# Loading one head of k first in a fused attention and mixer kernel: a smaller first load, a smaller memset, and the row chain put behind

## The chip, the cores and the metric

The kernel runs on one core of one Trainium2 chip. The metric is the device time of one execution in microseconds (us). Engines are called by their names in the profile: PE is TensorE's matmuls, PEld its weight loads, DVE is VectorE, ACT is ScalarE, POOL is GpSimd, SP is SyncE, which here only issues DMAs.

## The reference

Grouped-query attention over 8 batches, 16 query heads that share 4 key and value heads, 384 tokens of 64 elements; its output, turned to tokens by 1024, goes through a residual MLP mixer.

```python
scores = (1/sqrt(64)) * q @ k^T            # k, v repeated 4 times over the heads
attn   = softmax(scores)
x      = (attn @ v) as [8, 384, 1024]
a1  = alpha1 * x + beta1
tok = einsum('ts,bsd->btd', w_tok, a1)      # w_tok 384 x 384
u   = x + lam * tok
a2  = alpha2 * u + beta2
ch  = relu(a2 @ w_ch1) @ w_ch2              # 1024 -> 4096 -> 1024
out = u + lam * ch
```

All inputs and the output are float32.

## The kernel before, in words

The work is split by batch. Batch 0 goes through attention and token mixing alone, in a lead-in of some 36 us (`side(0)`), while weights are still being loaded; from then on TensorE works on the two large matmuls of one batch (or of two together) and takes the attention of a later batch in between. The order of instructions on every engine is the order in which the program writes them (`manual_schedule`): each engine takes its own from that one text, in that order, and an engine that waits holds up all that stands behind it on the same engine. The tile framework adds the semaphore waits.

The lead-in is what the change touches. Its pieces:

- **Warm-up.** `wtokT` is cleared by VectorE (L847), and PE multiplies it with itself (`warmup`, L844): nine matmuls of 384 columns before anything is loaded, three more after the first scores, one after the fourth. Their results are not used.
- **Loads.** SP issues, in this order: heads 0 and 1 of k (`load_k`, L150), the row alpha1 and the row lam (`load_row`, L869), heads 2 and 3 of k, then the rows beta1, alpha2 and beta2. ScalarE issues q of heads 0 to 3 in two halves (L879). GpSimd issues the other q heads (L884), v (L164), w_tok (L944) and, after those, the weights w_ch1 (L185). GpSimd's own row work (`split` for beta) and its copies of heads 2 and 3 stand behind the first two loads of w_ch1.
- **k.** `place_k` (L160) copies a head of k twice, side by side, into bf16. For heads 0 and 1 of batch 0 one copy is VectorE's and the other ScalarE's. `k_transpose` (L255 on PE, copied by VectorE at L257) turns a head of k into `kT`; `q_transpose` (L265, copied at L267) does the same for q, two heads to a pair.
- **Scores and exponentials.** `scores` (L279) fills a PSUM bank, of which there are two, in 18 steps of four 128 x 128 blocks for two heads each; ScalarE takes the exponential of each step (L288). Nine blocks make one pair of heads, so steps 0 to 2 need pairs 0 and 1 only, and step 4 is the first that needs pair 2 (its q and head 1 of k).
- **av.** `av_piece` (L315) multiplies by v; VectorE divides by the row sums (L320, L323).
- **Row chain.** VectorE multiplies alpha1 by lam (`scale_rows`, L903) and splits the product into bf16 parts (`split`, L911, L913, L919). `spread` (L396 on PE, copied to `vecs` by VectorE, L398) hands these rows to all 128 partitions, and `a1` (L334) multiplies x by them.
- **w_tok.** `wtok_transpose` (L369, copied by VectorE, L372) turns w_tok into `wtokT`, three blocks at a time; the third of them waits for a PSUM bank that the copy of the first one frees.

`at` in `side(0)` lists what follows each step of scores: the number is the step, and the pieces are written out in the order of the list.

Of the kernel before, what the change touches and what calls it, by code (L numbers as in the profile page):

```python
# [12 lines left out]
def kernel(  # L13
# [21 lines left out]
    nc = tc.nc  # L35
    f32 = mybir.dt.float32
# [7 lines left out]
    B, Hq, S, D = q.shape  # L44
    Hkv = k.shape[1]
# [3 lines left out]
    P = 128  # L49
    NST = S // P  # L50
# [30 lines left out]
    hTf = hT.rearrange("p n s -> p (n s)")  # L81
# [45 lines left out]
    wtokT = const.tile([P, NST, S], bf, tag="wtokT", name="wtokT")  # L127
# [5 lines left out]
    ks, k2s, qrs = {}, {}, {}  # L133

    def by_head(ap):
        return ap.rearrange("h (p st) d -> p h st d", st=NST)

    def k_tile(b):
        k2s[b] = sb.tile([P, Hkv, 2, NST, D], bf, tag="k2", name="k2", bufs=1)

    def load_k(b, hs=(0, 2)):
        if b > 1:
            k_tile(b)
            for a in range(2):
                nc.gpsimd.dma_start(out=k2s[b][:, :, a], in_=by_head(k[b]))
            return
        for h in hs:
            ks[b, h // 2] = t = hTf[:, 7680 + 384 * h:8448 + 384 * h].bitcast(f32).rearrange(
                "p (h st d) -> p h st d", h=2, st=NST)
            nc.sync.dma_start(out=t, in_=by_head(k[b, h:h + 2]))  # L150

    def place_k(b, i, hs=(0, 1)):
        if b not in k2s:
            k_tile(b)
        copies = [nc.gpsimd.tensor_copy] * 2
        if b == 1 or b == 0 == i:
            copies = (nc.vector.tensor_copy, nc.vector.tensor_copy if i else nc.scalar.copy)
        lo, hi = hs[0], hs[-1] + 1
        for a in range(2):
            copies[a](out=k2s[b][:, 2 * i + lo:2 * i + hi, a], in_=ks[b, i][:, lo:hi])  # L160
# [22 lines left out]
    def load_w1(c):  # L183
        w1_slots[c] = w1_free.pop(0)
        nc.gpsimd.dma_start(out=w1[:, w1_slots[c]], in_=w1src[:, :, c * CW * P:(c + 1) * CW * P])  # L185
# [5 lines left out]
    def bank(shape, tag, name, dtype=f32):  # L191
        if tag == "mm":
            return mms.tile(shape, dtype, tag="mm", name=name, bufs=2)
        return psum.tile(shape, dtype, tag=tag, name=name, bufs=2 if tag == "sc" else 1)
# [34 lines left out]
    def side(b):  # L229
# [172 lines left out]
        def add(f, *a):  # L402
            us.append(lambda: f(*a))
# [28 lines left out]
        if not first:  # L432
# [10 lines left out]
            if (b - NPL) // 2 > 0:  # L443
                at = {}
# [18 lines left out]
                **{39 + 4 * i - i // 2 * 2: [(turn, p)] for i, p in enumerate((5, 6, 7)) if by_pe(p)}}  # L463
        add(k_transpose, 0, 1)
        add(q_transpose, 0, 1, "av", "ACT")
        add(place_k, 0, 0, (1,))
        add(q_transpose, 1, 1, "tp")
        lower, upper = range(NP // 2), range(NP // 2, NP)
        ut = a2_transpose
        at = {0: [(warmup, 3), (scale_rows, 0), (split, 0, 1, 0)], 1: [(k_transpose, 1, 1)],  # L470
              2: [(q_transpose, 2, 2, "av"), (split, 0, 1, 1)], 3: [(warmup, 1)],
              4: [(av, 0)], 5: [(spread, lower, "tp"), (a1, 0)], 6: [(av, 1), (k_transpose, 2, 2, "tp")],
              7: [(q_transpose, 4, 2, "av"), (a1, 1)], 8: [(av, 2)],
              9: [(wtok_transpose, 0, "av"), (wtok_transpose, 1, "tp")],
              10: [(wtok_transpose, 2, "av"), (q_transpose, 6, 2, "mm"), (fill_h, 0)], 11: [(av, 3), (rows_r, "tp")],
# [363 lines left out]
    with tc.manual_schedule(engines=order):  # L839

        def warmup(n):
            warm = bank([P, 512], "mm", "warm")
            for _ in range(n):
                nc.tensor.matmul(out=warm[:, :S], lhsT=wtokT[:, 0, :P], rhs=wtokT[:, 1, :],  # L844
                                 start=True, stop=True)

        nc.vector.memset(wtokT, 0.0)  # L847
        warmup(9)
        load_k(0, [0])

        rows_f = hTf[:32, 9216:10496].bitcast(f32)
        rows_t = hTf[:32, 10496:11520].bitcast(f32)
# [15 lines left out]
        def load_row(i, ap, n=4):  # L868
            nc.sync.dma_start(out=rows_f[:n * NP, i * P:(i + 1) * P],  # L869
                              in_=bass.AP(tensor=ap.tensor, offset=ap.offset, ap=[[0, n], [P, NP], [1, P]]))  # L870

        load_row(0, moe_alpha1)
        load_row(3, moe_lam)
        load_k(0, [2])
        load_row(1, moe_beta1)
        load_row(2, moe_alpha2, 1)
        load_row(4, moe_beta2, 1)
# [5 lines left out]
        def load_q4(g):  # L883
            nc.gpsimd.dma_start(out=qgs[g], in_=q[0, g * G:(g + 1) * G].rearrange("h (p st) d -> p h st d", st=NST))  # L884
# [5 lines left out]
            nc.vector.memset(t[:, :, :, D:], 1.0)  # L890
        AX = mybir.AxisListType.X
        nc.vector.tensor_copy(out=ident_f, in_=ident)
        for i, m in enumerate(masks):
            nc.vector.tensor_reduce(out=m, in_=ident[:32, 8 * (i + 1):24 + 8 * (i // 2)], op=ADD, axis=AX)
        nc.vector.tensor_scalar(out=masks[2], in0=masks[2], scalar1=-1.0, scalar2=None, op0=MUL)
# [47 lines left out]
        load_q4(2)  # L943
        nc.gpsimd.dma_start(out=wtok_in, in_=moe_w_tok.rearrange("(p tt) s -> p tt s", tt=NST))  # L944
        load_q4(3)
        place_k(0, 0, (0,))
        load_w1(order1[0])
        load_w1(order1[1])
        place_k(0, 1)
        scale_rows(1, nc.gpsimd)  # L950
        split(1, 2, None, nc.gpsimd)
# [7 lines left out]
        for i, f in enumerate(side(0)):  # L959
            f()  # L960
            if i == 3:
                load_k(1)
# [16 lines left out]
        def put_flips(ps, phase, b, places):  # L979
            for u, m in zip(places, ((flip_k, b), *((flip_q, b, i, 2) for i in range(0, NP, 2)))):  # L980
                put(ps, phase, u, *m)

        turns, at = side(1)
        put_all(0, 0, turns)
        put_all(0, 1, at)
        put_flips(0, 1, 2, (34, 36, 37, 42, 43))

        put(0, 1, 45, load_next, 3)
        put_all(1, 0, side(2)[1], lambda u: int(1.5 * u))
        put_flips(1, 0, 3, (53, 55, 57, 59, 61))  # L990
        put_all(1, 1, side(3)[1])
# [68 lines left out]
```

## Time and profile before

| what | value |
|---|---|
| time, median of 3 runs | 739.87 us (739.78 to 740.77) |
| the profiled execution | 739.61 us |
| its span in the profile | 737.8 us |
| PE busy | 727.0 us, 99% |
| VectorE, ScalarE, GpSimd busy | 69%, 44%, 22% |
| first matmul on PE | 1.52 us |
| first exponential on ScalarE | 6.34 us |
| mean granted clock of TensorE | 1.00 |

A line of the timeline gives the start and the duration in us, the engine, the line of the kernel, the operation, what it writes and reads, its shape, and how many instructions were merged; in brackets stands the idle time of the engine just before and what ended it. A line of the waits gives the waiting engine and line, what it waited for, the sum in us, the number of waits and the longest. Ends of matmuls are modelled, and a q after an engine's name is its sequencer.

### The profile page before, as it was taken

Reading aid. Unit: us, or ns where it says so; the run is one execution under the profiler, and the core shown is the slowest. Engines: PE = TensorE matmul, PEld = TensorE weight load, DVE = VectorE, ACT = ScalarE, POOL = GpSimd, SP = SyncE. Lnnn points to the kernel's source line nnn. Section 1 sums busy time; section 2 is a strip of 40 time slices with the busy share of each in tenths; the row PEclk is TensorE's granted clock in tenths of the full one; section 3 lists DMA queues with packets and bytes.
Section 4 is the critical chain, followed back from the end, with each engine's and each line's share of the span. In section 5 each row is a group of like instructions: output and inputs, shape, how many; then the busy total and the mean of one; then the engine's idle time right before and its main releaser. Section 6 shows DMA issues by size and latency. Waiting matters only on the chain.

```text
span 737.8 us, 14477 instructions
## 1 busy us (share of the span) xinstructions
PE 727.0 (99%) x5710; PEld 418.6 (57%) x5769; DVE 512.0 (69%) x993; ACT 325.7 (44%) x469; POOL 164.0 (22%) x211
## 2 busy tenths in 40 slices
PE   8999999999999999999999999999999999999998
PEld 5866555666555566655555566655555556654444
DVE  7763366467587889749777988747958988762354
ACT  7632431554332566663334366664343266660000
POOL 9434221420000332301012244020002222000011
PEclk9999999999999999999999999999999999999999
DMA  9999999999999999999979999998989999837965
GB/s 188 194 202 200 207 217 179 186 198 181 219 264 260 183 226 223 249 262 215 284 186 224 178 176 165 190 250 199 276 236 167 217 149 144 149 136 241 289 184 107
DMA packets 218017, 151.31 MB, mean 205 GB/s; under 512 B 88661, under 2 KB 197061, under 8 KB 217949
## 3 DMA queue, kind: packets, MB, share of 16 engines
q0 software_dynamic: 120304, 64.60, 66.8%
q1 hardware_dynamic: 96956, 85.33, 41.5%
q8 instruction: 45, 0.74, 0.4%
q10 hardware_dynamic: 688, 0.46, 0.2%
q14 instruction: 24, 0.19, 0.1%
HBM read 154.84 MB, written 38.27 MB: 262 GB/s over the span
## 4 chain that ended last, share of the span: by engine, by line
PE 85%; DVE 6%; DMA 5%; issue 2%; POOL 2%; ACT 0%; DVEq 0%; POOLq 0%
PE C L789 25%; PE X L723 17%; PE h L532 10%; PE ch L570 10%; PE Y L723 8%; PE sc L279 4%; PE Z L723 4%; PE sc L315 3%; PE sc L340 3%; DMA q_raw<-in_q_dram 2%; DMA ops<-a 1%; DMA out_dram<-hT 1%; DVE xr L323 1%; DVE hT L826 1%; DVE xr L347 1%
## 5 line engine op out<-in xcount | busy, mean ns | idle before, releaser
L288 ACT ACTIVATE es<-sc 128x1024 bf16<-128x1024 f32 x126 | 121.4, 1024 | 154.6 <-PE sc L279 143.5
L789 PE MATMUL C<-w,arena 128*128 128x512 bf16 (+2 forms) x711 | 163.7, 372 | 1.6 <-issue 0.3
L789 PEld LDWEIGHTS <-arena 128*128 128x128 bf16 x1040 | 94.8, 98 | 100.5 <-issue 5.1
L728 ACT ACTIVATE hT<-X,bias 128x384 f32<-128x384 f32 x144 | 83.8, 582 | 63.8 <-PE X L723 56.8
L723 PEld LDWEIGHTS <-w 128*128 128x128 bf16 x768 | 75.1, 98 | 50.5 <-issue 0.7
L185 POOL DMA_DIRECT2D w<-in_moe_w_ch_dram x68 | 62.2, 926 | 125.4 <-PE Z L723 51.7
L570 PE MATMUL ch<-arena,hT 128*128 128x512 bf16 x366 | 87.9, 379 | 1.0 <-issue 0.3
L517 POOL DMA_DIRECT2D out_dram<-hT x33 | 28.8, 872 | 258.4 <-DVE hT L688 79.7
L532 PE MATMUL h<-ops,w 128*128 128x384 bf16 (+1 forms) x480 | 83.2, 327 | 0.4
L723 PEld LDWEIGHTS <-pad 128*128 128x128 bf16 x576 | 56.4, 98 | 37.2
L723 PE MATMUL X<-ops,w 128*128 128x384 bf16 x384 | 70.2, 326 | 0.0
L723 PE MATMUL X<-ops,pad 128*128 128x384 bf16 x384 | 70.2, 326 | 0.0
L789 PE MATMUL C<-pad,arena 128*128 128x512 bf16 (+2 forms) x288 | 69.5, 373 | 0.4
L532 PEld LDWEIGHTS <-w 128*128 128x128 bf16 x480 | 45.3, 98 | 30.1 <-issue 1.8
L570 PEld LDWEIGHTS <-hT 128*128 128x128 bf16 x384 | 34.7, 98 | 36.8 <-issue 2.5
L347 DVE TENSOR_TENSOR xr<-sc,xr 128x384 f32<-128x384 f32 x56 | 31.0, 553 | 24.2 <-PE sc L340 24.2
L315 PEld LDWEIGHTS <-es 128*128 128x128 bf16 x1008 | 38.2, 97 | 12.4
L340 PEld LDWEIGHTS <-wtokT 128*128 128x128 bf16 x576 | 37.5, 98 | 11.8 <-DVE a L330 0.8
L279 PE MATMUL sc<-qT,kT 64*128 64x384 bf16 (+2 forms) x576 | 41.9, 271 | 1.8 <-ACT hT L288 0.3
L320 DVE RECIPROCAL rinv<-sc 128x6 f32<-128x6 f32 x56 | 10.8, 192 | 44.3 <-PE sc L315 44.1
L315 PE MATMUL sc<-v,es 128*128 128x65 bf16 x1008 | 39.8, 193 | 0.0
L723 PE MATMUL Z<-ops,w 128*128 128x384 bf16 x192 | 39.0, 326 | 0.2
(138 smaller groups left out, 910.6 us busy)
## 6 DMA issues: line engine op xcount, KB each, us to landing
w<-in_moe_w_ch_dram POOLq DMA_DIRECT2D x68, 512.0 KB, 9.6
w<-w2s SPq DMA_DIRECT2D x60, 512.0 KB, 4.6
pad<-w2s SPq DMA_DIRECT2D x24, 512.0 KB, 7.4
out_dram<-xr SPq DMA_DIRECT2D x56, 192.0 KB, 5.3
out_dram<-hT POOLq DMA_DIRECT2D x33, 256.0 KB, 6.0
arena<-in_moe_w_ch_dram POOLq DMA_DIRECT2D x16, 512.0 KB, 20.0
w2s<-arena SPq DMA_DIRECT2D x28, 256.0 KB, 4.9
q_raw<-in_q_dram POOLq DMA_DIRECT2D x28, 192.0 KB, 9.7
```

Source lines behind the costliest of these rows:

```text
L185: nc.gpsimd.dma_start(out=w1[:, w1_slots[c]], in_=w1src[:, :, c * CW * P:(c + 1) * CW * P])
L279: nc.tensor.matmul(out=sc[:, hh, k % 4:k % 4 + n], lhsT=kT[r, 2 * p // G, BLK[hh][sk], :], rhs=qT[r, p, st:st + n, :], start=True, stop=True)
L288: nc.scalar.activation(out=e, in_=sc, func=EXP, scale=scale_qk)
L315: nc.tensor.matmul(out=av[:, hh, sq, :], lhsT=ess[k // 4][:, m % 2, k % 4, :], rhs=vb[:, sk, hk, :], start=(sk == 0), stop=(sk == NST - 1))
L340: nc.tensor.matmul(out=ps[:, tt, :], lhsT=wtokT[:, st, tt * P:(tt + 1) * P], rhs=a1s[p][:, st, :], start=(st == 0), stop=(st == NST - 1 an ...
L347: nc.vector.tensor_tensor(out=u, in0=ps, in1=u, op=ADD)
L517: nc.gpsimd.dma_start(out=at, in_=o, accum_op=ADD)
L532: nc.tensor.matmul(out=ps[:, :n], lhsT=w1[:, w1_slots[c], dt, j * P:(j + 1) * P], rhs=a2T[:, dt, :n], start=(dt == 0), stop=(dt == NDT - 1))
L570: nc.tensor.matmul(out=ps, lhsT=hT[:, nt, ms * P:(ms + 1) * P], rhs=w2[:, row(nt)[0], row(nt)[1], cs], start=(i == 0), stop=(i == NNT - 1))
L723: nc.tensor.matmul(out=ps, lhsT=tb[g, o][:, dt, e * P:(e + 1) * P], rhs=opb(LEFT1[o])[:, dt], start=(o in (1, 2, 7) and dt == 0), stop=(dt ...
L728: nc.scalar.activation(out=snap[o, e], in_=ps, func=IDENT, bias=hi if o == 5 else lo)
L789: nc.tensor.matmul(out=x, lhsT=hid[:, t, LEFT2[o], ms * P:(ms + 1) * P], rhs=rhs[:, t % 4 * 512 + c0:t % 4 * 512 + c1], start=((not last o ...
```

## The change

Four edits, all in the lead-in of batch 0:

1. Only the first third of `wtokT` is cleared by the memset, and the warm-up matmuls use that third for both operands; eight of them stand at the start in place of nine.
2. The first load of k holds head 0 alone. Head 1 gets a load of its own, behind the rows alpha1 and lam and ahead of heads 2 and 3.
3. The two copies of head 0 are written right behind the float copy of the identity, ahead of the small reductions that make the masks; the copies of head 1 stand behind both q transpositions, and both are VectorE's.
4. The first part of the row chain (`scale_rows` and the first half of `split`) is put from behind step 0 to behind step 1, after the transposition of head 1, and `spread` with the first `a1` from behind step 5 to behind step 6.

```diff
-    def load_k(b, hs=(0, 2)):
+    def load_k(b, parts=((0, 2), (2, 4))):
...
-        for h in hs:
-            ks[b, h // 2] = t = hTf[:, 7680 + 384 * h:8448 + 384 * h].bitcast(f32).rearrange(
-                "p (h st d) -> p h st d", h=2, st=NST)
-            nc.sync.dma_start(out=t, in_=by_head(k[b, h:h + 2]))
+        t = hTf[:, 7680:9216].bitcast(f32).rearrange("p (h st d) -> p h st d", h=Hkv, st=NST)
+        ks[b, 0], ks[b, 1] = t[:, :2], t[:, 2:]
+        for lo, hi in parts:
+            nc.sync.dma_start(out=t[:, lo:hi], in_=by_head(k[b, lo:hi]))
...
-            copies = (nc.vector.tensor_copy, nc.vector.tensor_copy if i else nc.scalar.copy)
+            copies = (nc.vector.tensor_copy, nc.vector.tensor_copy if i or hs == (1,) else nc.scalar.copy)
...
         add(k_transpose, 0, 1)
         add(q_transpose, 0, 1, "av", "ACT")
+        add(q_transpose, 1, 1, "tp")
         add(place_k, 0, 0, (1,))
-        add(q_transpose, 1, 1, "tp")
...
-        at = {0: [(warmup, 3), (scale_rows, 0), (split, 0, 1, 0)], 1: [(k_transpose, 1, 1)],
+        at = {0: [(warmup, 3)], 1: [(k_transpose, 1, 1), (scale_rows, 0), (split, 0, 1, 0)],
               2: [(q_transpose, 2, 2, "av"), (split, 0, 1, 1)], 3: [(warmup, 1)],
-              4: [(av, 0)], 5: [(spread, lower, "tp"), (a1, 0)], 6: [(av, 1), (k_transpose, 2, 2, "tp")],
+              4: [(av, 0)], 6: [(spread, lower, "tp"), (a1, 0), (av, 1), (k_transpose, 2, 2, "tp")],
...
-                nc.tensor.matmul(out=warm[:, :S], lhsT=wtokT[:, 0, :P], rhs=wtokT[:, 1, :],
+                nc.tensor.matmul(out=warm[:, :S], lhsT=wtokT[:, 0, :P], rhs=wtokT[:, 0, :],
                                  start=True, stop=True)
 
-        nc.vector.memset(wtokT, 0.0)
-        warmup(9)
-        load_k(0, [0])
+        nc.vector.memset(wtokT[:, 0, :], 0.0)
+        warmup(8)
+        load_k(0, ((0, 1),))
...
         load_row(0, moe_alpha1)
         load_row(3, moe_lam)
-        load_k(0, [2])
+        load_k(0, ((1, 2), (2, 4)))
...
         nc.vector.tensor_copy(out=ident_f, in_=ident)
+        place_k(0, 0, (0,))
...
         load_q4(3)
-        place_k(0, 0, (0,))
         load_w1(order1[0])
```

## The prediction

> **What bounds the kernel now.** I read the page first, then the chain of waits, then PE's waits, then the first 16 us of each engine in the timeline.
>
> ```profile
> PE 727.0 (99%) x5710; PEld 418.6 (57%) x5769; DVE 512.0 (69%) x993; ACT 325.7 (44%) x469; POOL 164.0 (22%) x211
> ```
>
> TensorE is busy 99% of 737.8 us, so only idle or slow time of PE can be won. All of PE's waits in the run:
>
> ```profile
> PE warm L844 <- DVE wtokT L847: 1.5, 1, 1.5
> ...
> PE sc L279 <- ACT hT L288: 0.3, 1, 0.3
> PE tp L369 <- DVE wtokT L372: 0.2, 1, 0.2
> PE sc L279 <- DVE xr L323: 0.2, 1, 0.2
> PE tok L344 <- DVE arena L387: 0.2, 1, 0.2
> ```
>
> Every one that matters lies in the first 20 us. By windows, PE is idle 2.15 us of 0 to 16, and 0.18 us of 16 to 40. So the end moves by what the last wait before the dense part moves: that of the third w_tok transposition (L369) at 15.56 for VectorE. VectorE's timeline says why:
>
> ```profile
> 5.94 0.56 DVE L267 CAST qT<-tp 128x384 bf16<-128x384 f32 x1 [0.47 <-PE tp L265]
> 7.20 0.28 DVE L903 TENSOR_TENSOR hT<-hT 32x128 f32<-32x128 f32 x1 [0.70 <-DMA hT<-in_moe_lam_dram]
> 7.51 0.65 DVE L911 CAST hT<-hT 32x128 bf16<-32x128 f32 x1
> 8.20 0.48 DVE L913 SCALAR_TENSOR_TENSOR hT<-hT,arena 32x128 f32<-32x128 bf16 x1
> 8.61 0.34 DVE L257 COPY kT<-tp 128x384 bf16<-128x384 bf16 x1
> 8.88 0.53 DVE L267 COPY qT<-tp 128x768 bf16<-128x768 bf16 x1
> ...
> 11.14 0.68 DVE L398 COPY vecs<-vec 128x512 f32<-128x512 f32 x1
> ...
> 15.16 0.61 DVE L372 COPY wtokT<-tp 128x384 bf16<-128x384 bf16 x2
> ```
>
> From 7.20, when the lam row lands, VectorE has no gap to 15.16: it, not PE or the load of k, sets the end of the lead-in. ScalarE runs beside it, nearly as tight: its exponentials follow one another from 6.34 at 0.92 us each. The first exponential is at the end of this chain:
>
> ```profile
> 1.52 3.06 PE L844 MATMUL warm<-wtokT 128*128 128x384 bf16 x9 [1.52 <-DVE wtokT L847]
> 4.38 0.53 PE L255 MATMUL tp<-ident,k 128*128 128x128 bf16 x3
> 4.70 1.20 PE L265 MATMUL tp<-hT,arena 128*128 128x128 f32 x6
> 5.91 0.39 PE L279 MATMUL sc<-qT,kT 64*128 64x384 bf16 x4
> ```
>
> **Step 1, start.** The memset of 576 words took 0.54 us, one of 256 words 0.27, one of 4 words 0.06: 192 words take about 0.22, so PE starts 0.32 us earlier (1.20). Eight warm-up matmuls at the 0.32 us step of before end at 3.74, against 4.38. The load of head 0 is half of one that landed after 3.1 us (3.85 by its last semaphore). Bounds: no gain (3.85) and half of it saved (about 3.05, as half of its packets had moved by 2.55 and the rest took 0.75). I take 3.1: its packets go out in order of head. Its copies (0.26 on VectorE, 0.35 on ScalarE, whose table load ends at 3.09) are then done by 3.5, hidden under the warm-ups; at the other bound they cost 0.5. So k is transposed at 3.74, a gain of 0.64.
>
> **Step 2, first exponential.** The clock record shows full clock from 5.00, 3.48 us after PE's first matmul, so from about 4.68 after. Three f32 transpositions of q at the slow clock (0.21 each, the last 0.42) begin at 4.06 and end near 4.9; q's first half landed at 4.17 and has fewer bytes ahead of it now. ScalarE's copy (0.48) ends at 5.41, scores begin at 5.46, the first exponential at 5.89 against 6.34: a gain of 0.45. ScalarE's second copy of k (0.35) goes, but it ended at 6.10, before scores were ready: nothing.
>
> **Step 3, head 1.** Its load is SP's fourth, issued near 2.87, just where heads 2 and 3 were (2.89), behind the same two rows. That one is the row to price it by. The semaphore records give 14 of its 16 parts by 6.43 and the last two at 6.95 and 7.50; the last parts of alpha and lam came at 6.79 and 7.10. On the slowest ring things land in order of issue, so head 1, half as long as that load, comes last between lam (7.10) and 7.50 less what starts earlier. Bounds: 4.7 (if the rings reach it before GpSimd's packets, from 3.9 on) and 7.4. I take 7.0, near the row.
>
> **Step 4, the new wait.** VectorE now stands at head 1's two copies, before lam's row chain; behind it are kT of head 1, the row chain, qT of pairs 2 and 3. On PE the transposition of head 1 waits for them, and all later scores behind it. In sum: copies 7.02 to 7.52 (2 x 0.25), transposition and its copy to kT 7.9 to 8.2, L903 8.2, cast 8.5, L913 8.75, qT 9.15 (before 8.88), if the cast takes its shorter time, 0.22 (9.34). The same cast took 0.65 at 7.51, ending just after GpSimd's first issue of w1 (7.16 to 8.09); at 8.5 it meets the second (8.04 to 8.96) and would end near 9.05. Then qT is at 9.45 and the fifth exponential, which needs it, 0.6 later.
>
> ```profile
> 7.16 1.80 POOL L185 DMA_DIRECT2D w<-in_moe_w_ch_dram  x2
> ```
>
> The two copies of k are casts of the same kind; beside GpSimd's earlier issues one took its plain 0.25 (5.22). Held as L911's was, until 8.1, the second copy would make the shift of the sum below 1.24 in place of 1.05. The Trainium skill, page SBUF — State Buffer, section SBUF: two separate sides, has a rule for that: VectorE and GpSimd share one port pair by an exclusive lock, held for a whole instruction. The trace of before agrees at 7.51 and not at 5.22; by the rule the sum is the 1.24, without it 0.77.
>
> **Step 5, spread.** The four matmuls L396 now come behind scores 6, which wait for the fifth exponential's end. Before, that exponential ran 9.99 to 11.03, and L396 ran ahead of it, at 10.65. So L398's copy (11.14) must wait: the fifth exponential's end, plus 0.32 for the scores, plus 0.43 until the copy. With head 1 early (exponential 9.55 to 10.6) this gives 11.37, later by 0.23 although all before it is earlier; left in its old place it would have been 10.87. With head 1 at 7.0 and the short cast: 11.9, or 0.77 late; with the long cast 12.2, 1.05 late. L398 heads the gapless stretch of VectorE, so this is also what the wait at 15.56 and the end move.
>
> **Small edits, at nothing.** Heads 2 and 3 and beta leave SP one issue (0.45) later: GpSimd takes them at 8.90 and 9.89, they landed by 7.50 and 8.2. The rows alpha2 and beta2 (landed by 8.7) are first read at 17.73. GpSimd's own order is the same. If such a cover were gone it would cost 0.3 at most, and GpSimd's row chain, which ends at 14.1, is first read at 16.73.
>
> **Sum.** Walking the three queues through with these durations, before's own order gives 15.56 for the third w_tok transposition, as the trace has it; the new order gives 16.0 to 16.8, most likely 16.5. The profiled execution took 739.61 (span 737.8, 1.8 around it), 0.26 under the median of 739.87. Shift +0.95, counted on the median: 740.8.
>
> **Rivals.**
> A, the forecast: head 1 lands after 6.6, +0.5 to +1.25. Chance 0.62.
> B, head 1 lands before 6.4: then only step 5 remains, +0.23 (0.39 if the first exponential comes at 6.05): 740.1. For it: the q packets are done earlier with 96 KB less in the way, and SP's next ones may pass before GpSimd's start. Against: heads 2 and 3. Chance 0.18.
> C, faster: the exponentials keep their 0.45 and L396 is not what VectorE waits for, because the casts run short throughout: -0.3 to -0.5, 739.4 to 739.6. It needs head 1 before 6.3 and the fifth exponential's end below 10.4, which ScalarE's steady 0.92 does not give. Chance 0.08.
> D, slower beyond measurement: PE's clock opens a stretch later, since idle work is shorter (2.54 us against 2.86) and what follows it is transpositions and waits. The rows: warm-ups step at 0.32 before 5.00 and at 0.16 after. If it opened another 3.48 us later (8.16), the 2.7 us of PE work from 5.46 on would run at half speed, half of it left over: +1.35 on top of A or B, from 741.4 to 742.2. It decides if PE stands still for some tenths before 4.7, as it would with head 0 at 3.85. Chance 0.09. The Trainium skill, TensorE: Matmul & The Clock Gate, section Part 4: PE-mode transpose, says that transposes do not count as busy in the same way for that gate, which speaks for D; the trace of before, with 0.6 us of transposes ahead of 5.00, cannot tell.
> E, that nothing moves (VectorE's gap takes up both): 739.7 to 740.0, chance 0.03.
>
> **Numbers.** A measurement of this kernel tells about 0.2% from no change, 1.48 us: 738.39 and 741.35. Faster by that is out of reach of every case (a gain of 0.64 is all that PE's start offers): 0.03. Slower takes D, A's upper end with a blocked copy and later rows: 0.20. Within: 0.77. The range 739.7 to 741.4 holds A, B and E, without C and most of D.
>
> **What would show it.** First warm-up at 1.2, transposition of k at 3.75, first exponential at 5.9 (steps 1, 2). VectorE idle before the copies of head 1 until about 7.0, named DMA of k (step 3); row chain after 8 (step 4). L398's first copy behind L396 at 11.4 or later, with PE as releaser (step 5); L369's third at 16.0 to 16.8. Wrong if head 1's copies start before 6.4 (then B), if L398 is before 11.14 (C), or if scores near 6 still step at the slow clock (D).

## The result, and the profile after

The changed kernel took 741.96 us (median of 11, 740.68 to 742.21) against 739.81 for the kernel before (11 runs, 739.31 to 741.30): ratio 1.0023, interval 1.0014 to 1.0032. That is 2.15 us slower, where 0.95 was forecast (740.8, range 739.7 to 741.4): the sign was right, the size lay outside the range. The profiled execution took 740.92, 1.31 more than the profiled one of before (739.61); most others took 741.7 to 742.2. The question is thus twofold: what the 1.31 are, and what the other executions have on top.

The engines' line of the page after; PE does the same work in a span of 739.1:

```profile
PE 726.9 (98%) x5709; PEld 418.5 (57%) x5768; DVE 511.8 (69%) x994; ACT 325.5 (44%) x468; POOL 163.8 (22%) x211
```

PE's waits after (us in total, times, longest): the wait for the first clear is shorter (1.5 before), and two new ones stand behind it, for head 1's copy and for the qT that VectorE then delivers late.

```profile
PE warm L844 <- DVE wtokT L847: 1.1, 1, 1.1
PE tp L255 <- DVE k L160: 0.7, 1, 0.7
PE sc L279 <- DVE qT L267: 0.6, 1, 0.6
...
PE tp L369 <- DVE wtokT L372: 0.3, 1, 0.3
```

PE's timeline after (start, length): k's transposes at 3.71, scores at 5.29, then the stall ahead of head 1's transposes.

```profile
1.12 2.74 PE L844 MATMUL warm<-wtokT 128*128 128x384 bf16 x8 [1.12 <-DVE wtokT L847]
3.71 0.50 PE L255 MATMUL tp<-ident,k 128*128 128x128 bf16 x3
...
5.29 0.40 PE L279 MATMUL sc<-qT,kT 64*128 64x384 bf16 x4
...
7.26 0.46 PE L255 MATMUL tp<-ident,k 128*128 128x128 bf16 x3 [0.65 <-DVE k L160]
```

VectorE's timeline after. It idles 1.13 for head 1's load, the row chain (L904, L912, L914) starts at 8.02 instead of 7.20, the cast L912 takes 0.66, and L398 comes at 12.21 instead of 11.14, after a wait for PE's L396.

```profile
6.94 0.43 DVE L160 CAST k<-hT 128x192 bf16<-128x192 f32 x2 [1.13 <-DMA hT<-in_k_dram]
7.75 0.36 DVE L257 COPY kT<-tp 128x384 bf16<-128x384 bf16 x1 [0.38 <-PE tp L255]
8.02 0.27 DVE L904 TENSOR_TENSOR hT<-hT 32x128 f32<-32x128 f32 x1
8.33 0.66 DVE L912 CAST hT<-hT 32x128 bf16<-32x128 f32 x1
9.02 0.51 DVE L914 SCALAR_TENSOR_TENSOR hT<-hT,arena 32x128 f32<-32x128 bf16 x1
9.46 0.54 DVE L267 COPY qT<-tp 128x768 bf16<-128x768 bf16 x1
...
12.21 0.69 DVE L398 COPY vecs<-vec 128x512 f32<-128x512 f32 x1 [0.32 <-PE vec L396]
...
16.20 0.61 DVE L372 COPY wtokT<-tp 128x384 bf16<-128x384 bf16 x2
```

The third w_tok transposition follows at 16.60, 1.04 later than before, as steps 3 to 5 had it.

**What happens after 16.6.** Matching each matmul of the two traces gives how late PE runs at any place. It is 1.04 late from 20 to 39 us; at 40.6 it regains 0.37; then it is 0.67 late up to 180, and 0.89 at the last matmul (0.18 of that is added at one group of scores, at 187.4; why, the trace does not show). From the last matmul to the end of the span after takes 4.00 us, before 3.58: another 0.42. 0.89 + 0.42 = 1.31, the whole difference of the two profiled executions. What is regained at 40.6 is mostly a wait of before that after no longer has, seen in the weight loads of PE's timeline of before:

```profile
40.60 0.44 PEld L532 LDWEIGHTS <-w 128*128 128x128 bf16 x4 [0.31 <-DVE hT L543]
```

**The tail.** At the end SyncE waits for a fixed list of semaphores, in order of number, about 0.06 us each. The DMAs that SyncE and ScalarE issue signal eight of them in turn. The kernel before issues 304, so the last store signals 118, the last number of the list; the extra load of k makes it 305, and the last store signals 107, the third place. SyncE then stands at 107 until this store has landed, and works off seven more of these waits behind it, 0.43 us in all. The group of these waits on SyncE in the last stretch, first before (736.6 to 737.08), then after (737.7 to 738.39):

```profile
L1055 SPq EVENT_SEMAPHORE  x2: 28/28/28, 736.7 to 736.9; - x2
```

```profile
L1055 SPq EVENT_SEMAPHORE  x8: 27/28/28, 737.8 to 738.2; - x8
```

Before, the two waits are those for the last two stores, and none stands behind the second. After, the first of the eight is the one for the last store, and seven follow.

### The profile page after: what moved, and what is told of

Read it like the earlier page. It is cut to its first block, busy times and chain, and to the rows that moved or that the text cites. A ratio compares the mean times of both kernels' runs of the same rounds, so it can differ in the third digit from the quotient of the medians.

```text
span 739.1 us, 14477 instructions
## 1 busy us (share of the span) xinstructions
PE 726.9 (98%) x5709; PEld 418.5 (57%) x5768; DVE 511.8 (69%) x994; ACT 325.5 (44%) x468; POOL 163.8 (22%) x211
## 4 chain that ended last, share of the span: by engine, by line
PE 88%; DVE 7%; issue 2%; DMA 2%; ACT 0%; SPq 0%; DVEq 0%
PE C L789 25%; PE X L723 17%; PE h L532 10%; PE ch L570 10%; PE Y L723 8%; PE sc L279 5%; PE Z L723 4%; PE sc L315 3%; PE sc L340 3%; DMA ops<-a 1%; DVE xr L323 1%; DVE xr L347 1%; DVE a1f L328 1%; DVE hT L826 1%; PE h L223 1%
## 5 line engine op out<-in xcount | busy, mean ns | idle before, releaser
L532 PE MATMUL h<-ops,w 128*128 128x384 bf16 (+1 forms) x480 | 83.1, 327 | 0.3
L532 PEld LDWEIGHTS <-w 128*128 128x128 bf16 x480 | 45.5, 98 | 29.6 <-issue 1.8
```

Of the source, the lines that this page charges most:

```text
L532: nc.tensor.matmul(out=ps[:, :n], lhsT=w1[:, w1_slots[c], dt, j * P:(j + 1) * P], rhs=a2T[:, dt, :n], start=(dt == 0), stop=(dt == NDT - 1))
```

## The experiments

Each kernel was timed in five rounds beside the kernel before on the same chip, whose median was 740.09, 740.01, 739.88, 739.80 and 740.19 in the five sets; a set is named by that number. The ratios are not those of the medians alone (in e_lane the medians give 1.0015, the ratio is 1.0006), and an interval reaches some 0.7 us or more to either side: two versions whose medians differ by less are not told apart. In the diffs, "at" is the table of step lists for batch 0.

**The changed kernel again (sets 740.09 and 739.88).**

> The changed kernel once more, to see which step the slower of its two groups of times (740.7 to 740.9 and 741.7 to 742.2) comes from. Theory lead-in (head 1 lands late, VectorE's chain is put back): the third L369 starts between 16.5 and 17.7, and a time of 742.0 goes with an L369 at 17.6 or later. Theory gate (PE's clock opens a stretch later in most executions): L369 later by about 1.2 with warm-up steps of 0.32 still seen after 5 us. Theory tail (what follows the last matmul): L369 at 16.6 as in the first profile and 1.2 us more behind the last matmul. Median 741.9 by all three.

742.04 (9 runs), ratio 1.0023, 1.0014 to 1.0033. In its trace (741.27) q's second half landed at 5.62 instead of 4.25, L904 took 0.59 and L912 0.76, and L398 came at 12.67.

> The changed kernel once more, beside the next three on the same chip: median 742.0 (741.7 to 742.2) against 740.0 of the kernel before. The trace tells which late execution it caught: by the clock theory an execution above 741.7 has its clock opened after 5.6 us, because a window of 3.41 us with an early stall of PE in it did not count as busy, or closed again for 3.41 us around 10 to 16 us.

742.41 (5 runs), ratio 1.0032, 1.0019 to 1.0045. The trace (742.42) did have its clock opened late, at 6.74; yet L398 was at 12.22 and PE only 0.61 late at 118 to 130. What made it late is a wait for a transpose by DMA, near 134:

```profile
PE h L532 <- DMA ops<-a: 1.5, 1, 1.5
```

So the late clock is not what this execution paid for. In these two traces the first exponential started at 6.64 and 6.57, later than the 6.34 of before, where the first profiled trace had 5.72.

**Head 1 behind head 0 (set 740.09).** `load_k(0, ((0, 1),))` becomes `load_k(0, ((0, 1), (1, 2)))`, and the later load keeps heads 2 and 3.

> Head 1's load directly behind head 0's, ahead of the two rows; all else as changed. Lands near 3.9 as both heads did before. Theory lead-in: VectorE no longer waits at 6.9, PE does not stand still before L255; the fifth exponential ends near 10.5 and L398 starts near 11.3 (before 11.14, changed 12.21), L369 near 15.75; time 740.0, about 1.9 under the changed kernel if the slow group goes with it, 0.9 if not. Theory gate: only 0.9 less than the changed kernel, 741.1. Theory tail: 741.1.

741.05 (12 runs), ratio 1.0017, 1.0007 to 1.0027: by the medians about 1 us less than the changed kernel, though the intervals overlap. The lead-in theory's own signs (L398 near 11.3, 740.0) failed; the time is that of the two others, 741.1. Head 1 lands at 3.85; the row chain is early, the cast short, and VectorE reaches L398 and waits for PE's L396:

```profile
8.08 0.21 DVE L912 CAST hT<-hT 32x128 bf16<-32x128 f32 x1
...
11.82 0.69 DVE L398 COPY vecs<-vec 128x512 f32<-128x512 f32 x1 [0.66 <-PE vec L396]
```

So with head 1 early L398 is still 0.68 later than before, where step 5 gave 0.23; PE is 0.66 late from 20 to 39. The clock opened at 6.44 in this trace, the first exponential started at 6.12 and the second at 7.23, so the fifth ended at 11.00 and not at 10.6.

**Both, and the spread alone (sets 740.09 and 740.01).**

```
-  6: [(spread, lower, "tp"), (a1, 0), (av, 1), ...
+  5: [(spread, lower, "tp"), (a1, 0)], 6: [(av, 1), ...
```

> As the run before, and spread with the first a1 back behind step 5. Theory lead-in: L396 no longer waits for the fifth exponential, L398 near 10.6 to 10.9, L369 near 15.0 to 15.3, time 739.3 to 739.6: 0.3 to 0.6 under the kernel before. If the place of spread costs nothing, as with head 1 early in the run before. Theory gate: 0.5 under the run before, but above the kernel before, near 740.6.

740.66 (11 runs), ratio 1.0014, 1.0003 to 1.0024; not told apart from the run before. L398 came at 11.80 (10.6 to 10.9 expected), without a wait, since VectorE's second copy of k (0.62) and L904 (0.60) were long in this trace.

> Edit: the changed kernel with the spread of the rows (and the row product behind it) back at step 5, ahead of the scores of step 6; head 1's load stays behind the two rows. Lead-in theory (my step 5: the spread behind scores 6 costs VectorE 0.77 to 1.05 against step 5, and the wait for head 1 the rest): L398 no longer waits for PE's rows (0.32 in the profile), it starts at 11.4 to 11.9 instead of 12.21, PE's third use of L369 comes 0.3 to 0.8 us earlier than at 16.6, and the median is 741.2 to 741.7. Rival (head 1's lateness sets all, VectorE reaches the spread no earlier): L398 at 12.2, median 742.0. Rival (the rows' matmuls stand in PE's queue ahead of scores 6 and wait for the late row chain): the scores of step 6 start over 0.3 later, median 742.0 to 742.5.

741.45 (11 runs), ratio 1.0011, 1.0002 to 1.0019; the median is in the lead-in theory's range. In the trace L912 took 1.13, so L398 came at 12.18, now with VectorE busy up to it, not waiting for PE. Of the expectation's signs, L398's place failed and the absent wait held.

**The clock (sets 740.09, 740.01, 739.88).** In e_warm10, `warmup(8)` becomes `warmup(10)`. In e_fill, step 1 gets `(warmup, 3)` ahead of head 1's transposes and step 3 has four in place of one. In e_late, the whole tile is cleared and nine idle matmuls run, as before.

> Ten idle matmuls at the start in place of eight, nothing else. They end 0.64 us later, so k is transposed at 4.35, still ahead of the wait for head 1 near 6.95 that sets what follows. Theory gate: the long mode goes, median 740.8 (1.1 less). Theory lead-in: no change, 741.9 within 0.3. Theory tail: no change.

742.16 (6 runs), ratio 1.0025, 1.0014 to 1.0036. More idle work brings nothing back. In its trace the clock opened at 5.53, closed at 12.35 and opened again at 15.77. The rows of three stretches there (us, busy time of PE, PEld, VectorE, ScalarE, GpSimd, granted clock, DMA share, GB/s):

```profile
5.50:12.30 6.80, 5.45 (x63) 2.84 (x63) 5.11 (x13) 5.72 (x7) 6.48 (x12) 1.00 1.44 197
12.40:15.70 3.30, 3.30 (x40) 2.50 (x40) 2.38 (x5) 2.01 (x3) 3.12 (x5) 0.50 1.36 213
15.80:20.00 4.20, 4.16 (x70) 2.70 (x66) 3.97 (x11) 4.09 (x5) 4.20 (x6) 1.00 1.46 198
```

PE runs at half clock for 3.41 us after it had stalled around 10. It ends 2.31 late at 20 to 39, although L398 at 12.81 alone would make 1.65.

> Edit: three more idle matmuls of 0.16 us at the head of step 1's list, where PE stood 0.65 us for head 1's cast, and three more at step 3 (four in all), where it then stood 0.61 us for qT's eviction; nothing else. Clock theory (PE's stalls between 6.6 and 10.1 us decide whether the clock's window counts as busy, so that it opens a window later or closes again for 3.41 us in part of the executions): the share of executions at 741.7 and above falls and the median goes from 742.0 to 741.1 to 741.5; no execution shows a mean clock of 0.998 or less. Lead-in theory alone (the lateness is that of head 1 and of VectorE's chain, the same in all executions): median 742.0 as before the edit, since the idle matmuls fit into the stalls. Cost theory (the idle matmuls push the scores back): up to +0.3, 742.3.

743.02 (10 runs), ratio 1.0036, 1.0023 to 1.0050: by the medians 3.0 us above the kernel before, where the changed kernel lay 1.95 to 2.53 above it in the other sets (the intervals overlap). No part of the time came back, against the clock theory. The trace (742.04) has head 1 landed at 7.32 and L398 at 13.15, and adds 0.29 near 134; where the other 1 us of this median comes from it does not show. That idle matmuls do not fit into a stall at the half clock (0.32 each) is a guess.

> Edit: the changed kernel with the whole warm-up tile cleared and nine idle matmuls, as before; the rest of the change stays. PE then reaches k's transposes at 4.38 instead of 3.71, when q's second half (landed at 4.25, in one trace at 5.62) is there, and does not stall ahead of 7.0. Clock theory (the early start of PE only moves stalls into the first windows and makes the clock open a window later in part of the executions): no execution of the late group, median 741.2 to 741.5, which is the kernel before plus 1.04 of lead-in plus 0.42 of tail, or less. Lead-in theory alone: the chain of VectorE is unchanged, median 742.0. If the early start was a gain: above 742.0, up to 742.3.

741.61 (11 runs), ratio 1.0024, 1.0015 to 1.0033; the changed kernel in this set took 742.41, with overlapping intervals. The median lies between those of the two theories. The late group is not gone: its own trace (742.33) opened the clock at 5.75, had L398 at 12.74 and waited 0.9 near 134.

**The tail (sets 740.01 and 739.80).** In e_lane, `load_k(1)` becomes `load_k(1, ((0, 4),))`, one load for two; in b_lane the kernel before gets one load more, for the same tensor.

> Edit: batch 1's k comes in one load instead of two (nothing else), so the kernel issues 304 loads from its hardware queues as the kernel before does, not 305. Tail theory: with 305, the last store signals semaphore 107, which SyncE waits for third at the end, with eight more waits of 0.06 us each behind it (last matmul to end 4.00 us in the changed kernel's profile); with 304 it signals the last number in the list, as before (3.58). So last matmul to end falls to 3.58 (+-0.03), the lead-in stays (third use of L369 at 16.6 to 17.0) and the median falls by 0.42 from 742.0 to about 741.6. Rival, the tail's 0.42 belongs to something else (output stores that land later): last matmul to end stays at 4.00 and the median at 742.0. Rival, the late start of batch 1's k costs: a wait of PE on k's transposes of batch 1 appears and the median rises.

741.10 (11 runs), ratio 1.0006, 0.9998 to 1.0015, 0.9 less than the changed kernel had in the other sets. From the last matmul to the end: 3.56. The median fell by more than the 0.42; the trace shows nothing but the tail that changed for good (its L398, at 12.67, is that of e_again), so the other half of the fall is open.

> Edit: the kernel before with heads 2 and 3 of batch 1's k in a load each, so 305 loads from the hardware queues instead of 304, nothing else. Tail theory: last matmul to end goes from 3.58 to 4.00 and the median from 740.0 to 740.4. Otherwise: 740.0.

740.55 (11 runs), ratio 1.0010, 1.0001 to 1.0019. From the last matmul to the end: 3.99, +0.41 with no other edit. (The rest of that trace's 0.94 is its lead-in: the clock opened at 7.52 and L398 came at 11.98.) So the tail goes with the count of loads, both ways. It does so in all 20 traces: 3.56 to 3.59 us with 304, 3.98 to 4.02 with 305.

**The transpose near 134 (set 739.80).** In SyncE's queue the second transpose of batch 2's q goes behind the last L362 of batch 1:

```
-  put_flips(0, 1, 2, (34, 36, 37, 42, 43))
+  put_flips(0, 1, 2, (34, 36, 42, 43, 44))
```

> Edit: in the changed kernel the second transpose of batch 2's q (L176) goes behind batch 1's last transpose of a2 (L362) in SyncE's queue instead of ahead of it, nothing else; L362 is issued 1.2 to 2.7 us earlier, about 126 instead of 127.5 to 128.5. Theory a (L532's wait for that transpose makes the upper group): the wait of L532 near 134 is gone or under 0.3, most executions fall to 741.0 to 741.5, median 741.3 (740.0 plus 1.0 of lead-in at most plus 0.42 of tail). Theory b (the clock): nothing changes, 742.0.

741.90 (9 runs, six of them above 741.6), ratio 1.0026, 1.0016 to 1.0036. The wait is gone from the trace (L362 issued at 126.74, against 128.05 in the trace that waited 1.5), and the late group is still there: theory a fails as the only cause. The profiled execution (741.73) was late in the lead-in instead. Its VectorE and GpSimd:

```profile
7.42 0.83 DVE L160 CAST k<-hT 128x192 bf16<-128x192 f32 x2 [1.28 <-DMA hT<-in_k_dram]
8.90 0.63 DVE L904 TENSOR_TENSOR hT<-hT 32x128 f32<-32x128 f32 x1
9.57 0.41 DVE L912 CAST hT<-hT 32x128 bf16<-32x128 f32 x1
...
13.14 0.69 DVE L398 COPY vecs<-vec 128x512 f32<-128x512 f32 x1 [0.40 <-PE vec L396]
```

```profile
7.05 1.82 POOL L185 DMA_DIRECT2D w<-in_moe_w_ch_dram  x2
8.86 1.04 POOL L160 CAST k<-hT 128x384 bf16<-128x384 f32 x2
```

Head 1 landed at 7.39; its first copy (0.67 for 0.25) lasted until the first issue of w1 had passed, and L904 met GpSimd's casts.

> Edit: the same move, and batch 1's k in one load (304 hardware loads, as before). Theory a with the tail: what is left is the lead-in alone, last matmul to end 3.58, median 740.7 to 741.0. Theory b: 741.1 to 741.6.

741.40 (8 runs), ratio 1.0022, 1.0012 to 1.0032, above what theory a gave. L398 at 13.46: head 1 landed at 7.17, its second copy took 0.71 and L904 1.24. Last matmul to end: 3.57.

> Edit: the kernel before with the same move of batch 2's second q transpose behind L362, nothing else. Theory a: its executions above 740.5 (8 of 33 in the last set but one) go as well, median 739.6 to 739.8. Theory b or no effect: 740.0. If q's later transpose is waited for by batch 2's scores: 740.2 or more.

739.86 (11 runs), ratio 0.9999, 0.9990 to 1.0008: no change in the median. All eleven lie at or below 740.25, against 3 of 28 above 740.6 for the kernel before; that is too few to call a gain.

**The early start alone (set 739.88).** The kernel before with one third cleared and eight, or ten, idle matmuls.

> Edit: the kernel before with the clear of one third of the warm-up tile and eight idle matmuls, nothing else of the change. PE reaches k's transposes at 3.71 instead of 4.38, with both heads of the first load still to land (about 4): it waits there and at q's second half. Clock theory: those stalls make the window that ends between 6.0 and 7.5 us too empty in part of the executions; the fast ones stay at 739.5 to 739.9, some go 1 us higher, median 740.2 to 740.7 against 740.0. My forecast's small-edit step (worth nothing, hidden by what lands): 739.9 to 740.1. If the early start is a gain by itself: 739.5 to 739.8.

740.41 (11 runs), ratio 1.0004, 0.9995 to 1.0013. The trace (739.67) has L398 at 10.62, 0.52 earlier than before, and PE is 0.35 early at 20 to 39; the wait at 40.6 takes it back.

> Edit: the kernel before with the clear of one third of the warm-up tile and ten idle matmuls, so that PE starts 0.40 us earlier but reaches k's transposes at the same 4.35 us. Clock theory: the clock opens up to 0.40 us earlier in all executions and no stall is added, so the median falls by 0 to 0.2 (739.8 to 740.0) with fewer executions above 741. Otherwise no change: 740.0.

740.59 (11 runs), ratio 1.0007, 0.9998 to 1.0016. Its trace (740.45) has L911 at 7.29 taking 1.63 us, across both issues of w1, and L398 at 12.00. Neither can be told from no change; none is a gain.

**The w1 loads out of the way (set 740.19).** `load_w1(order1[0])` and `[1]` go behind GpSimd's copies and row product, to the head of the loop that issues the others.

> Edit: the changed kernel with GpSimd's first two w1 loads behind its own copies and row product instead of ahead of them (GpSimd then issues nothing between 7.1 and 12 us), nothing else. Blocking theory: VectorE's L160, L904 and L912 take 0.25, 0.27 and 0.21 us (GpSimd's own casts may still cover one), so L398 starts at 11.4 to 11.9 instead of 12.21 to 13.46, the lead-in's lateness falls to 0.3 to 0.7 and the median to 740.9 to 741.5. Landing theory (head 1 and the rows set it): L398 at 12.2 or more, median 741.7 to 742.0. Cost: w1 lands 4 to 5 us later; if the first L532 (27 us) waits for it, 0.5 to 2 us on top, and the median says nothing by itself.

743.71 (5 runs), ratio 1.0049, 1.0035 to 1.0063. VectorE's copies and L904 are short, as the blocking theory had it, though L912 still took 0.43 beside GpSimd's copies; but head 1 landed at 7.83 in this trace:

```profile
7.85 0.43 DVE L160 CAST k<-hT 128x192 bf16<-128x192 f32 x2 [1.99 <-DMA hT<-in_k_dram]
...
9.04 0.27 DVE L904 TENSOR_TENSOR hT<-hT 32x128 f32<-32x128 f32 x1
9.34 0.43 DVE L912 CAST hT<-hT 32x128 bf16<-32x128 f32 x1
```

L398 came at 13.41, the clock closed at 8.27 for 3.41 us, and PE waited 0.9 at 43.6.

> Edit: the same move of the two w1 loads in the kernel before. Blocking theory: L911 takes 0.21 instead of 0.65 us, L398 starts at 10.6 to 10.9 instead of 11.14; PE waits less for it, median 739.4 to 739.8 against 739.8 to 740.0, so it may beat both kernels. Landing theory: 740.0. Cost: if the first L532 waits for w1, 740.5 to 742.

742.00 (10 runs), ratio 1.0024, 1.0015 to 1.0033. The signs of the blocking theory failed: L911 took 0.44 beside GpSimd's issue of q (6.40 to 7.19), L913 1.03 beside its copies, which had moved forward to 7.13 to 8.15, and L398 came at 11.24. PE waits at 42, at the place where it waited 0.31 before:

```profile
PE h L532 <- DVE hT L543: 1.6, 1, 1.6
```

**All the repairs together (set 740.01).** Head 1 behind head 0, the spread at step 5, batch 1's k in one load.

> Edit: the changed kernel with head 1's load right behind head 0's, the spread back at step 5, and batch 1's k in one load. If the parts add up (head 1's load and the spread together took 1.38 off the changed kernel in the last runs, the tail theory takes off 0.42 more), the median is 740.2 to 740.3, which cannot be told from the kernel before (740.1). Tail theory wrong: 740.66 again. If what is left of the change (the clear of a third, eight idle matmuls, the early transposes) is a gain: below 739.8.

740.95 (11 runs, 739.36 to 741.50), ratio 1.0006, 0.9997 to 1.0014. By the medians the parts do not add up (740.2 to 740.3 expected), though the interval does not exclude that they do. The trace (741.49) shows one way: q's second half lands at 5.37, PE stands for it, and the clock opens only at 10.42, so the scores take 0.61 instead of 0.40.

```profile
5.50 0.88 PE L265 MATMUL tp<-hT,arena 128*128 128x128 f32 x3 [0.68 <-DMA arena<-in_q_dram]
6.31 0.61 PE L279 MATMUL sc<-qT,kT 64*128 64x384 bf16 x4
```

No version was faster than the kernel before.

## Why the prediction was right or wrong

The direction came from the chain that was forecast, as the six traces below show it: head 1 late, VectorE's row chain behind it, the spread behind scores 6. Three terms failed. The extra load was put at nothing and costs 0.42 us at the end of the program. The sum took the lead-in as one number, L398 at 11.9 to 12.2, where traces have it at 12.21 to 13.46. And "Every one that matters lies in the first 20 us", said of PE's waits, left out the wait near 134 us, 1.69 us in one of three traces. What the slower executions have in common stays open.

**Steps 1 and 2, right in the profiled trace.** k is transposed at 3.71 (3.74 forecast), the first exponential starts at 5.72 (5.89), the clock opened at 4.46 (4.68). Head 0 landed at 3.14 (3.1). In the two other traces of the changed kernel the first exponential started at 6.64 and 6.57, with q's second half landed at 5.62 in the one and the clock open at 6.74 in the other: the 0.45 is not won in every execution. With head 1 late it bought nothing either: L398 came at 12.21 with the first exponential at 5.72, and at 12.22 with it at 6.57.

**Step 3, right in the profiled trace.** Head 1 landed at 6.92 (7.0), lam at 6.27, alpha at 5.71: in order of issue on the slowest ring. Over the traces that keep this order of loads it is 6.73 to 7.39, and 7.83 in e_w1. Rival B (before 6.4) did not occur in any of them; e_head1 shows that it is the place in the queue: issued at 1.19 the load lands at 3.85, issued at 2.83 at 6.92.

**Step 4, right in kind, short in size.** The copies, the row chain and the long cast came as told (L904 at 8.02 against 8.2, qT at 9.46 against 9.45). But I gave the hold by GpSimd to one cast, or one copy at most. In other traces it falls on L160 (0.67 in e_flips), L904 (0.63 there, 1.24 in e_flips_lane), L912 (1.14 in e_late) or two of them. By the Trainium skill, SBUF — State Buffer, section SBUF: two separate sides, for certain kinds of VectorE operation whichever of VectorE and GpSimd starts first holds the shared port pair for its whole instruction and the other fully blocks. The traces agree in part. Some held operations end just behind a GpSimd instruction (L160 of e_flips at 8.08, the first issue of w1 at 8.00), but L904 of the profiled trace took its plain 0.27 from 8.02 on, inside the second issue (7.92 to 8.87), and L904 of e_again took 0.59 and ended at 8.69, before that issue did (8.89). What decides whether an operation is held stays open.

**Step 5, right in its rule, short in size where it stands alone.** L398 was to come 0.75 behind the fifth exponential's end. In the six traces of the table below and in e_head1 it comes 0.81 or 0.82 behind it. In the profiled trace the fifth exponential is the first of this group on ScalarE; it ends at 11.39:

```profile
10.37 2.92 ACT L288 ACTIVATE hT<-sc 128x1024 bf16<-128x1024 f32 x3 [0.35 <-PE sc L279]
```

What the step had wrong is when that exponential ends. It does so at 11.39 to 12.65 in the six traces, and with head 1 early (e_head1) at 11.00, where 10.6 was forecast, so that L398 is 0.68 late where 0.23 was forecast.

**Small edits at nothing, wrong in one.** This is a step that failed. A load more is not free in its number: it moves the last store to another semaphore and the end by 0.42 us. I had asked of that load only who waits for its data. e_lane and b_lane show the term with both signs.

**The sum, wrong.** I read L398's lateness from one trace and counted it on the median. In the six traces that share the changed kernel's order up to 40 us, PE's lateness at 20 to 39 is L398's start less 11.16 us (before 11.14), so step 5's chain is what sets it; but L398 varies by more than I gave it (11.9 to 12.2). That the forecast hit the first trace is luck, since its 12.21 is the earliest of the six:

| trace | time | L398 | PE late at 20 to 39 | at 118 to 130 | at 150 to 180 | last matmul | tail |
|---|---|---|---|---|---|---|---|
| changed kernel | 740.92 | 12.21 | 1.04 | 0.67 | 0.67 | 0.89 | +0.42 |
| again | 741.27 | 12.67 | 1.52 | 1.19 | 1.19 | 1.24 | +0.39 |
| again, second | 742.42 | 12.22 | 1.06 | 0.61 | 2.30 | 2.40 | +0.40 |
| e_lane | 740.86 | 12.67 | 1.51 | 1.21 | 1.21 | 1.24 | -0.03 |
| e_flips | 741.73 | 13.14 | 1.98 | 1.67 | 1.66 | 1.71 | +0.40 |
| e_flips_lane | 741.42 | 13.46 | 2.29 | 1.75 | 1.76 | 1.80 | -0.02 |

In each row the last two columns add up, within 0.04, to the time above 739.61. The terms against the forecast's 0.95: lead-in, 1.18 as the mean of the column at 118 to 130 (0.61 to 1.75), after some 0.37 regained at 40.6 that I had not seen either; tail, 0.42, left out; the wait near 134, 1.69 in one of the three traces of the changed kernel (0.56 a piece), left out. 1.18 + 0.42 + 0.56 is 2.16, where the medians differ by 2.15; with so few traces that closeness is chance, and the shares are rough. A clock that shuts again, which no one of these six traces shows, is not in the sum.

I had read "Every one that matters lies in the first 20 us" from before's one trace. The transpose that L532 needs lands at 131.5 there, 1 us ahead of its use; in other traces it lands up to 136.1 (e_w1). The wait appeared in traces of seven other kernels of this study, among them b_w1, so it is not the change's alone (with SyncE's queue in its old order, 7 of 12 traces of kernels with the change show it, and 1 of 5 of the kernel before and its versions); what e_flips shows is that it can be removed without the median's falling. Whether the change makes it more frequent stays open, as does what the executions near 742.0 hold in common: a late L398, the wait near 134 or the clock. Each trace of a time above 741.7 shows at least one.

**Rival D, not what the traces of the changed kernel show, but not absent.** The clock did open late in one of them (6.74), which then was among the least late up to 130. It did cost elsewhere: in e_warm10, where it shut for a window, PE was 0.66 later than L398 alone would make it, and it was shut in parts of the lead-in of e_best and e_w1. The mean granted clock that is on record for each execution says more than the traces. A window of 3.41 us at half clock takes 0.0023 off it; the time ahead of the first opening does not count in it (e_best, open from 10.42, has 1.000). All 130 executions of the kernel before in the five sets have 0.999 or 1.000. Of the 25 of the changed kernel (the first measurement and the two repeats) two have 0.998 and five have 0.995 to 0.997, as e_warm10's trace has with its shut window (0.997). These seven took 741.96 to 743.29 us. So with the change the clock does shut again in part of the executions, a term that the forecast had only as a late opening; but of the 20 executions above 741.7 the other thirteen show no such loss, so it is not what they have in common. The rule of the Trainium skill, TensorE: Matmul & The Clock Gate, section Part 4: PE-mode transpose, that I weighed for D does not hold here: the window of e_lane that opened the clock, 3.61 to 7.02, was 94% busy, but only 42% with matmuls other than transposes, while 76% of those did not open it in b_lane (0.69 to 4.10).

## What to carry to other kernels

Count the loads as well as their bytes: in this program, whose end waits for semaphores in a fixed order, one load more cost 0.4 us far from where it stands. A sum from one profiled execution is a sum for that execution: where an operation meets another engine's issues, take the spread from several traces before counting it on the median. Moving a load from ahead of two small rows to behind them moved its issue from 1.19 to 2.83 us and its landing from 3.85 to 6.92. And look at the granted clock of every execution, not of the traced ones alone.

## What the runs showed of the hardware

- The clock goes by windows of 3.41 us with a phase that differs from one execution to the next: e_w1 had it open for 3.41 us and then shut for 3.41, e_warm10 open for 6.83 and then shut for 3.41. Reckoned from the matmul records, it opened at the end of a window that was at least 85% busy (the first openings of 20 traces, from 4.46 to 10.42 us) and stayed shut behind 80% and less; once open, it closed for one window behind 54% (e_w1) and 64% (e_warm10), and stayed open behind 64% and more in others (e_late, e_flips_lane). Transposes count as busy in this reckoning; without them the windows that opened it run from 40 to 90%, while b_lane's, which did not, had 76%.
- A cast on VectorE of 32x128 took 0.20 to 1.63 us. The long ones ran beside GpSimd's issues or its own copies, but not every one beside them was long (e_head1's L912 took 0.21 at 8.08).
- A DMA transpose of q (L176) took 1.22 to 3.61 us to issue over the 20 traces.
